# Attention scores in 32-row tiles without the q/k re-layout, hand-ordered attention engines, and a software-pipelined expert loop

## The chip, the cores and the metric

The kernel runs on one core of a Trainium2 chip. The core has TensorE (PE, with its weight loads PEld), VectorE (DVE), ScalarE (ACT), GpSimd (POOL) and SyncE (SP, which here only issues DMAs); 16 DMA engines serve all queues. Each engine works through its own instructions in order and waits on semaphores for the others. The metric is the device time of one execution in microseconds (us), lower is better.

## The reference

An attention layer with a sliding window feeds a mixture-of-experts layer.

- Attention: q, k, v are 8 x 8 x 576 x 64 (batch, head, position, depth), fp32. For each batch and head, `scores = q k^T / 8 - slope_h * |i - j|`, kept only where `0 <= i - j < 128`; softmax over j; times v. The result is laid out as 4608 tokens x 512.
- Experts: `y_dense = relu(x w1_dense) w2_dense` for every token; each token also goes to the one expert (of 8) with the largest gate logit, `y_moe = p_gate * (relu(x w1[e]) w2[e])`. The output is the sum, 4608 x 512 fp32.

## The kernel before

**Attention stage.** The work is cut into 16 units: a unit is one batch and four of its eight heads. Within a unit there are five key tiles of 128 positions. For key tile kj, `scores(u, kj)` puts the mask and bias into PSUM with a matmul against the identity (L266), adds q times k for the four heads (L275), and ACT takes the exponential into `p32` (L283). Scores are needed only for two query tiles, so a step is 4 heads x 256 queries = 1024 columns (768 and 256 for the last two key tiles). The values v and p are each split into a high and a low bf16 part: the high part of p is the upper half of its fp32 word, the low part `plo` is a DVE subtraction (L291). `attend(u, qi)` multiplies p by v in three products per head and key tile (L322) and DVE normalizes by the row sum, which comes from a column of ones in v (L330, L332). POOL casts the result to bf16 rows `xrow` (L342), PE transposes it (L350) and ACT copies it out (L357, L364).

Before its scores a unit needs q and k with depth on the partitions. POOL's queue loads q and k raw (L130), DVE transposes 32 x 32 blocks into `qs`, `ks` (L146), and SP's queue moves those in 16 DMAs per unit to `qT`, `kT` (L157), so that each head has its 64 depths on 64 neighbouring partitions. v comes over SP's queue (L138), ACT casts its high part (L167), POOL subtracts for the low part `vl` (L168).

After both units of a batch, `gate(b)` computes the expert choice of 576 tokens: PE products L378, L388, L419, L427 with some dozen DVE instructions of 40 columns between them (L396 to L447), and POOL scatters the rows by expert into DRAM (`xs_dram`, L456).

**Expert stage.** 43 blocks (NB) of 128 rows, each of one expert. Block j is fetched by POOL (L602), PE transposes it (L621), DVE copies (L625), PE makes the dense and the expert's first layer `hd` and `hm` (L630, L638; 8 matmuls of 512 columns), ACT applies relu (L646, L647), PE transposes the result (L651), DVE copies (L655, L656), PE makes the second layer `y` (L659, L667; 8 more), ACT copies it out (L675), and POOL scatters it to the output rows (L676). `tok_i` (L611), the output row numbers, needs the fetched block.

**What sets the order.** The program is written as a loop over steps with `LAG = 2` between `scores` and `attend`, but the order of each engine's instructions is chosen by a scheduler at compile time from the dependencies, within the buffer counts of the pools: two score buffers (`psum_sq`), two output buffers (`psum_ax`), four of `p32`. The two stages follow each other; the expert weights are loaded and cast by 18 DMAs of POOL's queue (L76) during attention.

The function, with the numbers that the profile uses:

Of the kernel before, what the change touches and what calls it, by code (L numbers as in the profile page):

```python
# [22 lines left out]
def kernel(  # L23
# [12 lines left out]
    nc = tc.nc  # L36
# [45 lines left out]
    kTs, vfs, vhs, lts = [], [], [], []  # L82
    for i in range(2):
        kT = persist.tile([P, 2, SP_], F32R, name=f"kT{i}")
        nc.gpsimd.memset(kT.bitcast(F32)[:, :, S:SP_], 0.0)
        kTs.append(kT)
        vf = persist.tile([P, NT, 4, D], F32, name=f"vf{i}")
        nc.gpsimd.memset(vf[TAIL:P, NT - 1, :, :], 0.0)
        vfs.append(vf)
        vh = persist.tile([P, NT, 4, D + 1], BF16, name=f"vh{i}")  # L90
        nc.gpsimd.memset(vh[:, :, :, D : D + 1], 1.0)
        vhs.append(vh)
# [6 lines left out]
    for i in range(1):  # L99
# [8 lines left out]
    ppool = ph1.enter_context(tc.tile_pool(name="ppool", bufs=4))  # L108
    xpool = ph1.enter_context(tc.tile_pool(name="xpool", bufs=2))
    gs = ph1.enter_context(tc.tile_pool(name="gs", bufs=3))  # L110
    psum_sq = ph1.enter_context(
        tc.tile_pool(name="psum_sq", bufs=2, space=bass.MemoryType.PSUM)
    )
    psum_ax = ph1.enter_context(
        tc.tile_pool(name="psum_ax", bufs=2, space=bass.MemoryType.PSUM)
# [9 lines left out]
    def load_unit(u):  # L125
        b, hq = divmod(u, HQ)
        hs = slice(4 * hq, 4 * hq + 4)
        for nm, src in (("q", q), ("k", k)):
            t = ld.tile([P, R, 2, 32], F32R, name=f"{nm}raw", tag=f"{nm}raw")
            nc.gpsimd.dma_start(  # L130
                out=t.rearrange("p r c d -> p (r c d)"),
                in_=src[b, hs].rearrange("h (p r) d -> (h p) (r d)", r=R),
            )
            raw[(nm, u)] = t
        vf = vfs[u % 2]
        for t in range(NT):
            rows = min(P, S - t * P)
            nc.sync.dma_start(  # L138
                out=vf[:rows, t, :, :],
                in_=v[b, hs, t * P : t * P + rows, :].rearrange("h p d -> p h d"),  # L140
            )

    def prep_qk(u, nm):
        t = raw.pop((nm, u))
        s = stg.tile([P, 2, S], F32, name=f"{nm}s", tag=f"{nm}s")
        nc.vector.transpose(  # L146
            out=s.rearrange("p c (x r) -> p r c x", r=R),
            in_=t.bitcast(F32),
        )
        if nm == "q":  # L150
            d = qtp.tile([P, 2, S], F32R, name="qT", tag="qT")
        else:
            d = kTs[u % 2]
        for g in range(4):
            pl, hh = divmod(g, 2)
            for c in range(2):
                nc.sync.dma_start(  # L157
                    out=d.bitcast(F32)[hh * D + 32 * c : hh * D + 32 * c + 32, pl, 0:S],
                    in_=s[32 * g : 32 * g + 32, c, :],
                )  # L160
        qkT[(nm, u)] = d

    def prep_v(u):
        vf = vfs[u % 2]
        vh = vhs[u % 2]
# [5 lines left out]
    load_unit(0)  # L171

# [37 lines left out]
    tok_c = consts.tile([P, NT], I32, name="tok_c")  # L210
    nc.gpsimd.iota(tok_c, pattern=[[P, NT]], base=0, channel_multiplier=1)
# [16 lines left out]
    mask = consts.tile([P, HQ, 2, 2, PW], BF16, name="mask")  # L228
    with tc.tile_pool(name="mk", bufs=1) as mk:
        d_i = mk.tile([P, PW], I32, name="d_i")  # L230
        nc.gpsimd.iota(d_i, pattern=[[1, PW]], base=0, channel_multiplier=-1)
        d_f = mk.tile([P, PW], F32, name="d_f")
        nc.vector.tensor_copy(out=d_f, in_=d_i)
        inv = mk.tile([P, PW], F32, name="inv")
        big = mk.tile([P, PW], F32, name="big")
        nc.vector.tensor_single_scalar(out=inv, in_=d_f, scalar=0.0, op=ALU.is_lt)
        nc.vector.tensor_single_scalar(
            out=big, in_=d_f, scalar=float(WINDOW - 1), op=ALU.is_gt
        )
        nc.vector.tensor_tensor(out=big, in0=inv, in1=big, op=ALU.add)  # L240
        nc.vector.tensor_scalar_mul(out=big, in0=big, scalar1=NEG_BIG)
        for h in range(H):
            hq, g = divmod(h, 4)
            pl, r = divmod(g, 2)
            slope = 2.0 ** (-8.0 * (h + 1) / H)
            nc.vector.scalar_tensor_tensor(
                out=mask[:, hq, r, pl, :],
                in0=d_f,
                scalar=-slope / SCALE,
                in1=big,  # L250
                op0=ALU.mult,
                op1=ALU.add,
            )


    pbuf = {}

    def scores(u, kj):
        hq = u % HQ
        k0 = kj * P  # L260
        nq = min(PW, S - k0)
        qT = qkT[("q", u)]
        kT = qkT[("k", u)]
        sq = psum_sq.tile([P, 2, 512], F32, name="sq", tag="sq")
        for r in range(2):
            nc.tensor.matmul(  # L266
                out=sq[:, r, 0 : 2 * nq],
                lhsT=ident_b,
                rhs=mask[:, hq, r, :, 0:nq],
                start=True,  # L270
                stop=False,
            )
        for pl in range(2):
            for r in range(2):
                nc.tensor.matmul(  # L275
                    out=sq[:, r, pl * nq : (pl + 1) * nq],
                    lhsT=kT[r * D : (r + 1) * D, pl, k0 : k0 + P],
                    rhs=qT[r * D : (r + 1) * D, pl, k0 : k0 + nq],
                    start=False,
                    stop=(pl == 1),  # L280
                )
# [7 lines left out]
        phi = p32.bitcast(BF16).rearrange("p r l (c t) -> p r l c t", t=2)[:, :, :, :, 1]
        plo = ppool.tile([P, 2, 2, PW], BF16, name="plo", tag="plo")  # L290
        nc.vector.tensor_tensor(  # L291
            out=plo[:, :, :, 0:nq],
            in0=p32[:, :, :, 0:nq],
            in1=phi[:, :, :, 0:nq],
            op=ALU.subtract,
        )
        pbuf[(u, kj)] = (phi, plo)
# [3 lines left out]
    def attend(u, qi):  # L301
        b, hq = divmod(u, HQ)
        rows = min(P, S - qi * P)
        vh, vl = vparts[u]
        ax = psum_ax.tile([P, 512], F32, name="ax", tag="ax")
        ax_v = ax[:, 0 : 4 * (D + 1)].rearrange("p (h d) -> p h d", h=4)
        for g in range(4):
            pl, r = divmod(g, 2)
            kl = [kj for kj in (qi - 1, qi) if kj >= 0]
            n = 0  # L310
            for kj in kl:
                phi, plo = pbuf[(u, kj)]
                c0 = 0 if qi == kj else P
                hi = phi[:, r, pl, c0 : c0 + rows]
                lo = plo[:, r, pl, c0 : c0 + rows]
                for lhs, rhs, w in (
                    (hi, vh[:, kj, g, :], D + 1),
                    (hi, vl[:, kj, g, :], D),
                    (lo, vh[:, kj, g, :], D + 1),
                ):  # L320
                    n += 1
                    nc.tensor.matmul(  # L322
                        out=ax_v[:rows, g, 0:w],
                        lhsT=lhs,
                        rhs=rhs,
                        start=(n == 1),
                        stop=(n == 3 * len(kl)),
                    )
        recip = gs.tile([P, 4], F32, name="recip", tag="recip")
        nc.vector.reciprocal(out=recip[:rows], in_=ax_v[:rows, :, D])  # L330
        xf = xpool.tile([P, 4, D], F32, name="xf", tag="xf", bufs=4)
        nc.vector.tensor_tensor(  # L332
            out=xf[:rows],
            in0=ax_v[:rows, :, 0:D],
            in1=recip[:rows].unsqueeze(2).to_broadcast([rows, 4, D]),
            op=ALU.mult,
        )
        if hq == 0 and qi == 0:
            cur["xT"] = xpool.tile([P, 4, SP_], F32, name="xT", tag="xT", bufs=1)
            cur["xrow"] = xpool.tile([P, NT, RW], BF16, name="xrow", tag="xrow", bufs=2)  # L340
        xT, xrow = cur["xT"], cur["xrow"]
        nc.gpsimd.tensor_copy(  # L342
            out=xrow[:rows, qi, hq * 256 : hq * 256 + 256],
# [370 lines left out]
```

## Time and profile before

| | |
|---|---|
| median of 3 runs | 598.61 us (597.23 to 600.31) |
| profiled execution | 603.1 us, span 601.4 us |
| busy in the span: PE / DVE / ACT / POOL | 76% / 50% / 32% / 45% |
| mean granted TensorE clock | 0.807 of 2.4 GHz |
| DMA | 76.36 MB, 127 GB/s over the span |

The span is the time between the first and the last instruction; the execution's own time is 1.7 us more. The busy share is an average over two very different stages: attention (to about 362 us) and the experts (from about 380 us). The stages have to be read apart.

### The profile page before, as it was taken

What the parts mean: (1) busy time and instruction counts of PE and PEld (TensorE: products, weight loads), DVE (VectorE), ACT (ScalarE), POOL (GpSimd) and SP (SyncE); (2) the same over time, 40 slices, a digit from 0 to 9 for tenths busy, and PEclk for the clock granted to TensorE, in tenths of its full rate; (3) what the DMA queues carried; (4) which work ended last, traced back from release to release, by engine and by line L of the source; (5) the groups of instructions that cost most, each with busy time, mean ns of one, the idle gap of its engine ahead of it and who ended that gap; (6) DMA issues with size and microseconds to landing.
All of it is one profiled execution on the core that took longest, in us unless ns stands there. A gap on an engine that the chain in (4) does not pass through costs nothing. (4 is left out here: it accounts for less than half of the span.)

```text
span 601.4 us, 10655 instructions
## 1 busy us (share of the span) xinstructions
PE 456.5 (76%) x3828; PEld 272.7 (45%) x3828; DVE 303.2 (50%) x554; ACT 193.0 (32%) x298; POOL 271.2 (45%) x366
## 2 busy tenths in 40 slices
PE   0476566977776776777778782699999999999992
PEld 0254343654544554545555461344444444444440
DVE  3746456687588668766786755122222222222220
ACT  1222223343134233432441431233333333333331
POOL 6362565474274264454552623544434444444432
PEclk9995666756776776676677696699999999999997
DMA  7899999785576557657556401121121211222110
GB/s 186 212 235 221 249 249 239 189 213 117 137 204 137 147 150 165 163 119 188 161 137 139 119 2 41 45 81 58 70 69 60 80 67 71 69 80 78 55 52 26
DMA packets 72418, 76.36 MB, mean 127 GB/s; under 512 B 46252, under 2 KB 55470, under 8 KB 72368
## 3 DMA queue, kind: packets, MB, share of 16 engines
q0 software_dynamic: 21408, 47.35, 30.6%
q1 hardware_dynamic: 50960, 28.35, 20.3%
q8 instruction: 31, 0.51, 0.4%
q14 instruction: 19, 0.16, 0.1%
HBM read 52.93 MB, written 16.06 MB: 115 GB/s over the span
## 5 line engine op out<-in xcount | busy, mean ns | idle before, releaser
L291 DVE TENSOR_TENSOR plo<-p 128x1024 bf16<-128x1024 f32 (+2 forms) x80 | 108.8, 1398 | 15.2 <-ACT p L283 15.2
L283 ACT ACTIVATE p<-sq 128x1024 f32<-128x1024 f32 (+2 forms) x80 | 66.3, 852 | 98.1 <-PE sq L275 87.4
L322 PE MATMUL ax<-vh,plo 128*128 128x65 bf16 (+1 forms) x576 | 89.0, 225 | 11.1 <-DVE plo L291 11.1
L625 DVE COPY xT<-xps 128x512 bf16<-128x512 bf16 x43 | 18.2, 423 | 156.2 <-PE xps L621 152.7
L322 PEld LDWEIGHTS <-p 128*128 128x128 bf16 (+1 forms) x1152 | 84.0, 122 | 23.6 <-issue 20.6
L266 PE MATMUL sq<-mask,ident_b 128*128 128x512 bf16 (+2 forms) x160 | 60.8, 478 | 42.0 <-ACT p L283 20.9
L322 PE MATMUL ax<-vh,p 128*128 128x65 bf16 (+1 forms) x576 | 90.4, 226 | 0.0
L322 PE MATMUL ax<-vl,p 128*128 128x64 bf16 (+1 forms) x576 | 89.9, 224 | 0.0
L342 POOL CAST xrow<-xf 128x256 bf16<-128x256 f32 (+1 forms) x80 | 44.4, 559 | 79.8 <-DVE xf L332 79.7
L322 PEld LDWEIGHTS <-plo 128*128 128x128 bf16 (+1 forms) x576 | 68.4, 122 | 22.6 <-DVE plo L291 17.8
L350 PE MATMUL tp<-ident_f,xf 128*128 128x128 f32 (+1 forms) x160 | 42.0, 354 | 43.1 <-DVE xf L332 42.4
L675 ACT COPY yo<-y 128x512 f32<-128x512 f32 x43 | 25.2, 585 | 131.0 <-PE y L667 124.9
L275 PE MATMUL sq<-qT,kT 64*128 64x256 f32 (+2 forms) x320 | 60.3, 405 | 6.1 <-DMA kT<-ks 4.4
L456 POOL DMA_INDIRECT xs_dram<-xrow,slot x40 | 46.5, 1164 | 33.2 <-DVE slot L441 14.1
L676 POOL DMA_INDIRECT out_dram<-yo,tok_i x43 | 43.6, 1014 | 36.9 <-issue 14.7
L275 PEld LDWEIGHTS sq<-qT,kT 64*128 64x128 f32 x320 | 42.2, 262 | 28.9 <-issue 20.5
L630 PE MATMUL hd<-w_all,xT 128*128 128x512 bf16 x172 | 52.3, 387 | 0.9 <-DVE xT L625 0.5
L168 POOL TENSOR_TENSOR vl<-vf,vh 128x1280 bf16<-128x1280 f32 x16 | 45.7, 2856 | 16.0 <-ACT vh L167 15.9
L602 POOL DMA_INDIRECT xr<-xs_dram,row_i x43 | 43.9, 1021 | 16.0 <-issue 14.7
L357 ACT COPY xT<-tp 128x512 f32<-128x512 f32 x32 | 18.7, 586 | 86.5 <-PE tp L350 86.5
L638 PE MATMUL hm<-w_all,xT 128*128 x172 | 45.0, 385 | 0.0
L659 PE MATMUL y<-w_all,hT 128*128 128x512 bf16 x172 | 44.1, 379 | 0.5 <-DVE hT L655 0.5
(109 smaller groups left out, 607.4 us busy)
## 6 DMA issues: line engine op xcount, KB each, us to landing
qraw<-in_q_dram POOLq DMA_DIRECT2D x16, 576.0 KB
kraw<-in_k_dram POOLq DMA_DIRECT2D x16, 576.0 KB
qT<-qs SPq DMA_DIRECT2D x128, 72.0 KB
kT<-ks SPq DMA_DIRECT2D x128, 72.0 KB
vf<-in_v_dram SPq DMA_DIRECT2D x64, 128.0 KB
w_all<-in_moe_w_dram POOLq DMA_DIRECT2D x16, 512.0 KB
vf<-in_v_dram SPq DMA_DIRECT2D x16, 64.0 KB
w_all<-in_moe_w_dense_dram POOLq DMA_DIRECT2D x2, 512.0 KB
```

What stands on the lines that cost most here:

```text
L168: nc.gpsimd.tensor_tensor(out=vl, in0=vf, in1=vh[:, :, :, 0:D], op=ALU.subtract)
L266: nc.tensor.matmul(out=sq[:, r, 0 : 2 * nq], lhsT=ident_b, rhs=mask[:, hq, r, :, 0:nq], start=True, stop=False,)
L275: nc.tensor.matmul(out=sq[:, r, pl * nq : (pl + 1) * nq], lhsT=kT[r * D : (r + 1) * D, pl, k0 : k0 + P], rhs=qT[r * D : (r + 1) * D, pl, k ...
L283: nc.scalar.activation(out=p32[:, :, :, 0:nq], in_=sq[:, :, 0 : 2 * nq].rearrange("p r (l c) -> p r l c", l=2), func=ACT.Exp, scale=SCALE,)
L291: nc.vector.tensor_tensor(out=plo[:, :, :, 0:nq], in0=p32[:, :, :, 0:nq], in1=phi[:, :, :, 0:nq], op=ALU.subtract,)
L322: nc.tensor.matmul(out=ax_v[:rows, g, 0:w], lhsT=lhs, rhs=rhs, start=(n == 1), stop=(n == 3 * len(kl)),)
L342: nc.gpsimd.tensor_copy(out=xrow[:rows, qi, hq * 256 : hq * 256 + 256], in_=xf[:rows].rearrange("p h d -> p (h d)"),)
L456: ins = nc.gpsimd.indirect_dma_start(out=xs_dram[:, :], out_offset=bass.IndirectOffsetOnAxis(ap=slot[:rows, t : t + 1], axis=0), in_=xrow_ ...
L602: nc.gpsimd.indirect_dma_start(out=xm_i[:, :], out_offset=None, in_=xs_dram[:, :], in_offset=bass.IndirectOffsetOnAxis(ap=row_i[:, j : j + ...
L630: nc.tensor.matmul(out=hd, lhsT=xT[:, kc, :], rhs=w_all[:, E, 0, kc, :], start=(kc == 0), stop=(kc == 3),)
L638: nc.tensor.matmul(out=hm, lhsT=xT[:, kc, :], rhs=w_all[:, bass.DynSlice(er, 1), 0, kc, :], start=(kc == 0), stop=(kc == 3),)
L659: nc.tensor.matmul(out=y, lhsT=hT[:, c, :], rhs=w_all[:, E, 1, c, :], start=(c == 0), stop=False,)
```

## The change

**Layout of q and k.** The 16 re-layout DMAs per unit go. A head's 64 depths are now summed in two passes over 32 partitions (c = 0, 1), with head g on partitions 32g to 32g+31, which is where the DVE transposes leave them; ACT copies `ks` to `kT` and `qs` to `qT` (L159, L167 of the new file). So that the tokens of one q tile fall into place, q is loaded in five DMAs, and q, k and v all come over SP's queue. The queries of a tile stand in another order, so the mask and the token numbers `tok_c` are built for that order.

**Two key tiles per step.** A unit has three steps, key tiles (0,1), (2,3) and (4). A step's scores go to two PSUM tiles `sq0`, `sq1` of two heads each, without a second buffer; the exponential and `plo` are done per pair of heads over 1024 columns. The normalization handles two query tiles at once (`ax`, one buffer). v's high part is read in place as the upper half of its fp32 word, and DVE makes `vl` (L174).

**Order by hand.** PE, ACT and DVE follow the order of the code in the attention stage. A step n is: scores of n, exponentials, `plo` of the first head pair, products and normalization of step n-1, `plo` of the second pair, then the transposes of the next unit's k (first step), q (second step) or v's low part (third step). `gate` is cut in three and spread over three steps.

**Expert loop.** PE, ACT, DVE and POOL follow the code. PE takes `turn_h(j)`, `layer1(j+1)`, `turn_x(j+2)`, `layer2(j)`; blocks are fetched four ahead; DVE instead of ACT copies `y` out.

On ACT, in one unit of attention, the scheduler's order before (five exponentials of a unit, the cast of v and a copy):

```order
L283 ACTIVATE p_2829<-sq 128x1024
L283 ACTIVATE p_2883<-sq 128x1024
L283 ACTIVATE p_2985<-sq 128x1024
L167 CAST vh_75<-vf_73 128x20x64
L283 ACTIVATE p_3033<-sq 128x4x192
L283 ACTIVATE p_3086<-sq 128x4x64
L357 COPY xT<-tp 128x2x2x128 x2
```

and the written order now, the three steps of a unit:

```order
L346 ACTIVATE p_1254<-sq_1232 128x1024
L346 ACTIVATE p_1257<-sq_1233 128x1024
L448 COPY xT<-tp 128x2x2x128
L159 CAST kT_70<-ks 128x2x576
L346 ACTIVATE p_1328<-sq_1306 128x1024
L346 ACTIVATE p_1331<-sq_1307 128x1024
L448 COPY xT<-tp 128x2x64
L167 CAST qT<-qs 128x1152
L346 ACTIVATE p_1403<-sq_1389 128x2x64
```

The casts of the next unit's k and q now stand between the exponentials of one step and those of the next.

On DVE, in a unit of attention, before (both transposes, then `plo` of three key tiles):

```order
L146 STREAM_TRANSPOSE ks<-kraw 128x18x64
L146 STREAM_TRANSPOSE qs<-qraw 128x18x64
L291 TENSOR_TENSOR plo<-p_2587 128x1024
L291 TENSOR_TENSOR plo<-p_2641 128x1024
L291 TENSOR_TENSOR plo<-p_2686 128x1024
L330 RECIPROCAL recip<-ax 128x4
L332 TENSOR_TENSOR xf<-ax,recip 128x256
```

and now (the first step and the second; the names p_1254 to p_1331 are those of the exponentials shown above):

```order
L365 TENSOR_TENSOR plo<-p_1254 128x1024
L410 RECIPROCAL recip<-ax 64x4
L412 TENSOR_TENSOR xf<-ax,recip 64x256
L365 TENSOR_TENSOR plo<-p_1257 128x1024
L157 STREAM_TRANSPOSE ks<-kraw 128x18x64
L365 TENSOR_TENSOR plo<-p_1328 128x1024
L410 RECIPROCAL recip<-ax 128x8
L412 TENSOR_TENSOR xf<-ax,recip 128x512
L365 TENSOR_TENSOR plo<-p_1331 128x1024
L165 STREAM_TRANSPOSE qs<-qraw 128x18x2x32
L365 TENSOR_TENSOR plo<-p_1403 128x2x64
```

The transpose of k has moved between the last `plo` of one step and the first of the next, that of q one step later.

On POOL, in the expert loop, before (`xr` with a number is one of five buffers of fetched blocks):

```order
L602 DMA xr_85<-xs_dram,row_i 128x260
L611 TENSOR_TENSOR tok_i<-xr_85,inval_i 128x1
L676 DMA out_dram<-yo,tok_i 4608x512
L602 DMA xr_77<-xs_dram,row_i 128x260
L611 TENSOR_TENSOR tok_i<-xr_77,inval_i 128x1
```

and now:

```order
L727 DMA xr_75<-xs_dram,row_i 128x260
L793 TENSOR_TENSOR tok_i<-xr_81,inval_i 128x1
L826 DMA out_dram<-yo,tok_i 4608x512
L727 DMA xr_77<-xs_dram,row_i 128x260
L793 TENSOR_TENSOR tok_i<-xr_83,inval_i 128x1
```

Before, `tok_i` reads the block whose fetch stands directly ahead of it; now one that was fetched three iterations earlier.

The diff, cut to its core:

```diff
 def load_unit(u):
...
+        t = ld.tile([P, R, 2, 32], F32, name="qraw", tag="qraw")
+        for i in range(NT):
+            n = 4 if i < NT - 1 else 2
+            nc.sync.dma_start(
+                out=t[:, 4 * i : 4 * i + n, :, :].rearrange("p r c d -> p (r c d)"),
+                in_=q[b, hs, i * P : i * P + 32 * n, :].rearrange(
+                    "h (p r) d -> h p (r d)", r=n),
+            )
...
-        for g in range(4):
-            pl, hh = divmod(g, 2)
-            for c in range(2):
-                nc.sync.dma_start(
-                    out=d.bitcast(F32)[hh * D + 32 * c : hh * D + 32 * c + 32, pl, 0:S],
-                    in_=s[32 * g : 32 * g + 32, c, :],
-                )
+    def transpose_k(u):
+        s = stg.tile([P, 2, S], F32, name="ks", tag="ks")
+        nc.vector.transpose(out=s.rearrange("p c (x r) -> p r c x", r=R), in_=t)
+        d = kTs[u % 2]
+        nc.scalar.copy(out=d[:, :, 0:S], in_=s)
...
-        nc.scalar.copy(out=vh[:, :, :, 0:D], in_=vf)
-        nc.gpsimd.tensor_tensor(out=vl, in0=vf, in1=vh[:, :, :, 0:D], op=ALU.subtract)
+        nc.vector.tensor_tensor(
+            out=vl, in0=vf[:, :, :, 0:D], in1=vh[:, :, :, 0:D], op=ALU.subtract)
...
+        for i, kj in enumerate(kjs):
+            nq = min(wid, S - kj * P)
+            for c in range(2):
+                for g in range(4):
+                    nc.tensor.matmul(
+                        out=sq[g // 2][:, g % 2, i * wid : i * wid + nq],
+                        lhsT=kT[32 * g : 32 * g + 32, c, kj * P : kj * P + P],
+                        rhs=qT[32 * g : 32 * g + 32, c, kj * P : kj * P + nq],
+                        start=False, stop=(c == 1 and i == len(kjs) - 1))
...
+    for n in range(NS + 6):
+        if n < NS:
+            lo = scores(u, pr)
+            lo(0)
+        if 1 <= n <= NS:
+            norms[n - 1] = attend(*steps[n - 1])
+            flips[n - 1] = norms.pop(n - 1)()
+        if lo is not None:
+            lo(1)
...
+            flip(*steps[n - 2], flips.pop(n - 2))
...
+            if pr == 0:
+                load_v(u + 1)
+                transpose_k(u + 1)
+            elif pr == 1:
+                transpose_q(u + 1)
+            else:
+                prep_v(u + 1)
+                if u + 2 < NU:
+                    load_unit(u + 2)
...
-            nc.scalar.copy(out=yo, in_=y)
+            nc.vector.tensor_copy(out=yo, in_=y)
...
+        AHEAD = 4
+        for j in range(AHEAD):
+            fetch(j)
+        turn_x(0)
+        layer1(0)
+        turn_x(1)
+        for j in range(NB):
+            turn_h(j)
+            if j + 1 < NB:
+                layer1(j + 1)
+            if j + 2 < NB:
+                turn_x(j + 2)
+            layer2(j)
+            if j + AHEAD < NB:
+                fetch(j + AHEAD)
```

## Rows read from the trace of the kernel before

**Rows 1.** Windows: stretch, length, busy of PE, PEld, DVE, ACT, POOL, clock, DMA, GB/s.
```profile
60.00:100.00 40.00, 25.29 (x236) 16.94 (x235) 21.05 (x39) 10.86 (x17) 22.91 (x28) 0.60 1.19 250
150.00:200.00 50.00, 37.45 (x404) 26.34 (x405) 35.75 (x58) 15.48 (x23) 21.12 (x28) 0.69 0.64 157
450.00:500.00 50.00, 48.36 (x290) 22.86 (x289) 11.78 (x30) 18.31 (x32) 21.77 (x30) 1.00 0.19 66
```

**Rows 2.** Timeline of DVE: k transposed, first and last of ten units.
```profile
140.77 2.34 DVE L146 STREAM_TRANSPOSE ks<-kraw 128x1152 f32<-128x1152 f32 x1
...
327.17 2.33 DVE L146 STREAM_TRANSPOSE ks<-kraw 128x1152 f32<-128x1152 f32 x1
```

**Rows 3.** Timeline of DVE: start and end of attention.
```profile
17.14 2.77 DVE L246 SCALAR_TENSOR_TENSOR mask<-d_f,big 128x256 bf16<-128x256 f32 x8
...
28.36 2.33 DVE L291 TENSOR_TENSOR plo<-p 128x1024 bf16<-128x1024 f32 x2
...
361.45 0.17 DVE L330 RECIPROCAL recip<-ax 64x4 f32<-64x4 f32 x1 [0.71 <-PE ax L322]
361.73 0.42 DVE L332 TENSOR_TENSOR xf<-ax,recip 64x256 f32<-64x256 f32 x1
```

**Rows 4.** Line L291: durations in ns, min/median/max over all its forms.
```profile
L291 DVE TENSOR_TENSOR plo<-p x80: 414/1208/4489, 28.4 to 358.0; 128x1024 bf16<-128x1024 f32 x48, 128x768 bf16<-128x768 f32 x16, 128x256 bf16<-128x256 f32 x16
```

**Rows 5.** Lines by form: busy us, mean ns of one, idle before.
```profile
L283 ACT ACTIVATE p<-sq 128x1024 f32<-128x1024 f32 x48 | 47.4, 1022 | 47.4 <-PE sq L275 43.5 <-ACT p L283 2.0 <-issue 2.0
...
L146 DVE STREAM_TRANSPOSE ks<-kraw 128x1152 f32<-128x1152 f32 x16 | 37.4, 2339 | 6.0 <-DMA kraw<-in_k_dram 5.7
...
L167 ACT CAST vh<-vf 128x1280 bf16<-128x1280 f32 x16 | 20.1, 1255 | 14.0 <-DMA kT<-ks 14.0
...
L283 ACT ACTIVATE p<-sq 128x256 f32<-128x256 f32 x16 | 6.1, 383 | 36.3 <-PE sq L275 32.1 <-DVE xf L332 2.4 <-DVE plo L291 1.9
...
L396 DVE TENSOR_REDUCE mx<-lg 128x5 f32<-128x40 f32 x8 | 1.6, 200 | 11.4 <-PE lg L388 11.4
```

**Rows 6.** Timeline of PE: four 64-row score matmuls; sixteen 32-column gate matmuls.
```profile
353.01 0.50 PE L275 MATMUL sq<-qT,kT 64*128 64x256 f32 x4
...
160.24 1.18 PE L378 MATMUL lp<-xT,wg_pad 128*32 128x288 f32 x16
```

**Rows 7.** Timeline, DVE and POOL: a plo beside POOL's vl.
```profile
147.37 3.55 DVE L291 TENSOR_TENSOR plo<-p 128x1024 bf16<-128x1024 f32 x1
...
146.53 3.32 POOL L168 TENSOR_TENSOR vl<-vf,vh 128x1280 bf16<-128x1280 f32 x1 [0.40 <-ACT vh L167]
```

**Rows 8.** Timeline of PE in the expert loop, one block and the next.
```profile
481.27 0.40 PE L651 MATMUL hps<-ident_b,hr 128*128 128x128 bf16 x4
...
483.01 1.03 PE L659 MATMUL y<-w_all,hT 128*128 128x512 bf16 x4
483.87 1.03 PE L667 MATMUL y<-w_all,hT 128*128 x4
...
487.82 1.03 PE L659 MATMUL y<-w_all,hT 128*128 128x512 bf16 x4
```

**Rows 9.** Timeline of POOL in the expert loop, from one output scatter to the next.
```profile
482.19 1.01 POOL L676 DMA_INDIRECT out_dram<-yo,tok_i  x1 [0.58 <-ACT hr L647]
...
486.36 0.18 POOL L611 TENSOR_TENSOR tok_i<-xr,inval_i 128x1 int32<-128x1 int32 x1 [1.83 <-DMA xr<-xs_dram,row_i]
487.12 1.02 POOL L676 DMA_INDIRECT out_dram<-yo,tok_i  x1 [0.58 <-ACT hr L647]
```

**Rows 10.** Timeline, PE and POOL: first and last work of the expert loop.
```profile
379.98 0.61 PE L621 MATMUL xps<-ident_b,xr 128*128 128x128 bf16 x4 [13.09 <-DMA xr<-xs_dram,row_i]
...
589.52 1.03 PE L667 MATMUL y<-w_all,hT 128*128 x4
...
588.98 0.98 POOL L676 DMA_INDIRECT out_dram<-yo,tok_i  x1 [2.51 <-DMA out_dram<-yo,tok_i]
...
597.87 0.98 POOL L676 DMA_INDIRECT out_dram<-yo,tok_i  x1 [4.52 <-issue]
```

More of the change, by code (lines that the diff above doesn't have):

```diff
@@ L289, in scores @@
[L289 to L297, printed above, removed]
-    cur = {}
[L301 to L343, printed above, removed]
-            in_=xf[:rows].rearrange("p h d -> p (h d)"),
-        )
-        if qi % 2 == 0:
-            cur["tp"] = psum_m.tile([P, 2, 2, P], F32, name="tp", tag="misc")
-        tp = cur["tp"]
-        for c in range(2):
-            nc.tensor.transpose(
-                out=tp[:, qi % 2, c, 0:rows],
-                in_=xf[:rows, 2 * c : 2 * c + 2, :],
-                identity=ident_f[:rows, :rows],
-            )
-        if qi % 2 == 1:
-            q0 = (qi - 1) * P
-            nc.scalar.copy(
-                out=xT[:, 2 * hq : 2 * hq + 2, q0 : q0 + PW].rearrange(
-                    "p c (t x) -> p t c x", t=2
-                ),
-                in_=tp,
-            )
-        elif qi == NT - 1:
-            nc.scalar.copy(
-                out=xT[:, 2 * hq : 2 * hq + 2, qi * P : qi * P + rows],
-                in_=tp[:, 0, :, 0:rows],
-            )
@@ new lines, in scores @@
+        ps = []
+        for i in range(2):
+            p32 = ppool.tile([P, 2, 2 * PW], F32, name="p32", tag="p32")
+            nc.scalar.activation(
+                out=p32[:, :, 0:tot],
+                in_=sq[i][:, :, 0:tot],
+                func=ACT.Exp,
+                scale=SCALE,
+            )
+            phi = p32.bitcast(BF16).rearrange("p g (c t) -> p g c t", t=2)[:, :, :, 1]
+            plo = ppool.tile([P, 2, 2 * PW], BF16, name="plo", tag="plo")
+            ps.append((p32, phi, plo))
@@ new lines, in flip @@
+    def flip(u, pr, xf):
+        b, hq = divmod(u, HQ)
+        qis = KP[pr]
+        rows = P if len(qis) == 2 else TAIL
+        nt = len(qis)
+        if hq == 0 and pr == 0:
+            cur[("xT", b)] = xpool.tile([P, 4, SP_], F32, name="xT", tag="xT", bufs=1)
+        xT = cur[("xT", b)]
+        tp = psum_m.tile([P, 2, 2, P], F32, name="tp", tag="misc")
+        for i in range(nt):
+            for c in range(2):
+                nc.tensor.transpose(
+                    out=tp[:, i, c, 0:rows],
+                    in_=xf[:rows, i, 2 * c : 2 * c + 2, :],
+                    identity=ident_f[:rows, :rows],
+                )
+        q0 = qis[0] * P
+        nc.scalar.copy(
+            out=xT[:, 2 * hq : 2 * hq + 2, q0 : q0 + nt * rows].rearrange(
+                "p c (t x) -> p t c x", t=nt
+            ),
+            in_=tp[:, 0:nt, :, 0:rows],
+        )
@@ L467, in gate @@
             tc.add_to_no_dep_group(scat_group, ins.ins)
-    steps = [(u, kj) for u in range(NU) for kj in range(NT)]
-    prep_qk(0, "q")
-    prep_qk(0, "k")
+    sch = ph1.enter_context(
+        tc.manual_schedule(
+            engines={
+                mybir.EngineType.PE,
+                mybir.EngineType.Activation,
+                mybir.EngineType.DVE,
+            }
+        )
+    )
+    steps = [(u, pr) for u in range(NU) for pr in range(3)]
+    transpose_k(0)
+    transpose_q(0)
@@ L472 @@
     prep_v(0)
     load_unit(1)
[L474 to L495 removed]
+    norms, flips, later = {}, {}, {}
```

426 lines of the change are left out of this document (281 added, 145 removed).

## The prediction, made before the changed kernel ran

> **What bounds the kernel now.** I read the windows first, because the span falls into two stages that no mean describes. In the expert loop PE works 48.4 of 50 us at a granted clock of 1.00; in attention 37.5 of 50 us at 0.69, with DVE at 35.8 and no engine full [rows 1]. Only the lower and the upper level (1.2 and 2.4 GHz) are granted there, in turn.
>
> Then the timeline. In the expert loop the y matmuls of one block start 4.81 us after those of the block before [rows 8]. The whole loop runs from 379.98 to 590.55 us, 210.6 us [rows 10]: 43 blocks x 4.81 = 206.8, and 3.8 to fill it. POOL is as slow as PE there: from one output scatter to the next are 4.93 us, because `tok_i` waits for the block whose fetch was issued just ahead of it [rows 9], and at the end POOL is behind, with its last scatter at 597.87 us, 7.3 us after PE's last matmul [rows 10].
>
> In attention the transposes of k mark the units: nine units in 186.4 us, 20.7 us each [rows 2]. The first `plo` begins at 28.36 us and the last normalization ends at 362.15 [rows 3].
>
> The profiled execution took 603.1 us (span 601.4), the median of the runs shown is 598.6, 4.5 less. I make the sum on the profiled execution and take the difference over to the runs.
>
> **The expert loop, the surest part.** Its matmuls are the same before and after: 16 of 512 columns per block and 12 transposes. Four y matmuls take 0.86 us from start to start (483.01 to 483.87), so one takes 0.216; four transposes take 0.40 us, of which the last one alone shows 0.22, so one takes 0.06 [rows 8]. 16 x 0.216 + 12 x 0.06 = 4.18 us of PE in a block of 4.81: 0.63 us are waits for relu and for copies. In the new order every such wait has other work in front of it: relu of block j+1 has `turn_x` and `layer2(j)` (0.24 + 1.73 us) against the two relus that follow the last matmul of the layer by less than 1 us; the DVE copy of `turn_h(j)` has `layer1(j+1)` (1.73 us). On DVE a block's copies are about 0.8 + 0.4 + 0.7 us, on ACT only the two relus are left. On POOL the `tok_i` wait goes; what is late next there is the chain of output scatters, each of which waits for the landing of the one before: 2.51 + 0.98 = 3.49 us where they follow one another closely [rows 10], less than 4.2. I take 4.2 us per block and 4.5 to fill (one stage more): 43 x 4.2 + 4.5 = 185.1, a gain of **25.5 us**. Bounds: 0 if something else keeps 4.8 us; 27 if no wait is left.
>
> The tail: now 10.8 us pass between PE's last matmul and the end of the span (590.55 to 601.4), since POOL is behind. If it isn't behind, there remain a copy (0.7), a scatter and what follows a last scatter now (597.87 to 601.4, 3.5 us): about 5, or up to 9 if the 4.52 us of "issue" before the last scatter [rows 10] come again. I take 6, a gain of **5 us**.
>
> **Attention, where the gain is doubtful.** What goes: 16 re-layout DMAs per unit and POOL's `vl`. With `vl` goes a wait: a `plo` beside it took 3.55 us [rows 7] against a median of 1.21 [rows 4]. What comes: two ACT casts of 1152 columns per unit, `vl` on DVE, and a fixed order. The fixed order makes a chain that can be followed: DVE transposes k, then ACT casts it, and only behind this cast stands the next step's first exponential, for which DVE's next `plo` waits. I add one unit up along DVE, with handovers of 0.06 us:
>
> - First step: `plo` 1.21; normalization 0.70 (reciprocal start to the end of xf, 361.45 to 362.15 [rows 3]); `plo` 1.21; transpose of k 2.34 [rows 5]: 5.5. Then DVE waits for the cast, 1.15 (estimate from 1.255 for 1280 columns), and the exponential, 1.02 [rows 5], with handovers 2.3.
> - Second step: `plo` 1.21; normalization of 512 columns instead of 256, about 1.0; `plo` 1.21; transpose of q 2.34: 5.8. Wait for the cast and a small exponential (0.28, estimate from 0.383 for 256 columns): 1.5.
> - Third step: two small `plo` 0.3 each, normalization 1.0, `vl` 1.5 (estimate from 1.21 for 1024 columns): 3.1. Meanwhile PE makes the next scores, which had to wait until ACT had emptied `sq0` and `sq1`, as these have no second buffer: four mask matmuls (0.9 at the upper clock, twice that at the lower), four rounds of scores (1.0 to 2.0) and the exponential 1.02: 2.9 to 4.8. DVE waits up to 1.7; I take 0.8.
> - The gate: 13 DVE instructions of about 0.2 us [rows 5] per two units and some waits: 1.5 per unit. POOL's cast beside `vl`: 0.2.
>
> The sum is 20.7 us, and about 20.5 if back-to-back `plo` overlap a little: what the unit takes now. The removed DMAs and the smaller number of instructions are paid back by 3.8 us of new waiting behind the casts. Bounds of one unit: 18 (no wait after the third step, faster casts) and 22.5.
>
> What hides the other edits: q's five loads and v's five are 0.6 us each to issue on SP, which loses 16 issues per unit. PE's fp32 transposes and products are the same in number; they stand in the shadow of DVE's transposes. v's high part is now read with a stride of two bf16: if that slowed the products, some 2 us per unit of PE, this would be hidden there too, except in the third step.
>
> Total: the first exponential had to wait for q and k through SP's DMAs; now the masks are last (8 of 512 columns instead of 256: 5 us instead of 2.77 [rows 3]), so the first `plo` comes at about 24 us instead of 28.4 (between 21 and 29). Units 0 and 1 have no gate before them: 2 x 19; units 2 to 14: 13 x 20.5 = 266.5; the last has nothing to prepare: 10.7. Sum 315, so the end is at 339. While the expert weights stream in, DMA is full (share 1.19, [rows 1]); all 18 are now issued from the start, beside the loads that the transposes need. I add 6 us: 345 instead of 362.15, a gain of **17 us** (bounds: 40, and a loss of 20).
>
> Gate, routing and first fetch, 17.8 us between 362.15 and 379.98, stay.
>
> **Sum.** 25.5 + 5 + 17 = 47.5: 603.1 becomes 555.6, and the runs 598.6 become **551**.
>
> **A rule weighed.** The four tiles must work at the same time. The trace has two tiles of 64 rows: four matmuls of 256 columns in 0.50 us, while one alone shows 0.4; and sixteen gate matmuls that use 32 columns of the array each in 1.18 us [rows 6], four at a time. So I count a round of four like a round of two, 0.25 us. The Trainium skill (TensorE: Matmul & The Clock Gate, "Measured speedup vs the span model") gives 3.07 times, not 4, for four row tiles. By that a round would take 0.33 us; only the four rounds after the third step are exposed, 0.3 us per unit and 5 us in all: 556. No run here shows it yet.
>
> **The rivals.**
>
> *Faster attention (14%).* ACT's and DVE's pieces are shorter than my estimates and PE is granted the upper clock, so that the third step's wait vanishes: 18.4 us per unit, 15 x 2.1 = 31 us more: 520. For it: DVE and ACT together are far from full [rows 1]. Against: the order is a chain, not a load.
>
> *Loads late (16%).* While weights stream, q and v of the next unit are late; DVE stands in the transpose with everything behind it. Five units at 5 us more: 576. For it: the DMA share of 1.19 and PE at only 25 of 40 us in that stretch [rows 1]. Against: k, q and v no longer share POOL's queue with the weights, and no re-layout competes.
>
> *The expert loop stays (8%).* The change doesn't do what it says: the scatter chain or the register loads for the expert number keep 4.8 us per block: 25.5 and the tail come back, 582. Against: 3.49 us per scatter.
>
> *Slower: the tiles take turns (7%).* If the four row tiles run one after another, a round of 0.25 us becomes 1.0 and the 10 rounds of a unit cost 7.5 us more of PE at the upper clock, 15 at the lower. PE has about 5 of 20.7 us free now (37.5 of 50 busy, [rows 1]). So a unit gets 2.5 to 10 us longer; with 6, 15 x 6 = 90 us: 641. It decides from 3.2 us per unit on, where the 47.5 are used up. Against: rows 6.
>
> **How the numbers follow.** The forecast has 55%, with a range of its own of 537 to 567 (a unit of 19.7 to 21.5). With most of the cases at 520, 576 and 582 the range of 8 in 10 is 521 to 582. The measurement can tell about 0.5% (3 us) from no change. Faster: 55 + 14 + 16 + 8 less the ends of the wide cases, 91%; same 2%; slower 7%.
>
> **What would show it.** In the new profile: y matmuls of successive blocks 4.2 us apart; PE's last matmul within 6 us of the end; ks transposes 20.5 us apart; between a transpose of k and the next `plo` about 2.3 us in which ACT does a cast and an exponential; four score matmuls of 256 columns in 0.25 to 0.35 us at the upper clock. I am wrong if DVE waits for DMA in steady units, if PE's rounds take turns, or if the unit is under 19 us.

## The result, and the profile after

The changed kernel takes 563.07 us (median of 4 runs, 560.39 to 563.8), the kernel before 598.5: a ratio of 0.940 (95% interval 0.936 to 0.944). The forecast was 551 us, with a range of 521 to 582. The time lies in the range, 12 us above the point. One run of an experiment below (the new loop under the old attention, 579.0 us) fell in a slower state of the chip and is left out of its time.

The profiled execution took 560.4 us (span 558.7). Cut at the same places as the forecast:

| stretch | forecast, us | measured, us |
|---|---|---|
| start to the first `plo` | 24 | 28.0 |
| units 0 and 1 | 38 + 6 for loads | 63.8 |
| units 2 to 13, each | 20.5 | 18.7 |
| unit 14 and the last | 31.2 | 29.6 |
| end of attention at | 345 | 345.65 |
| gate, routing, first fetch | 17.8 | 18.35 |
| expert loop | 185.1 | 184.6 |
| PE's last matmul to the end | 6 | 10.05 |

The end of attention was met to 0.65 us, and not because its terms were right: the first units are 20 us too long, the steady ones 22 us too short.

The windows of the changed kernel (columns as in [rows 1]), a stretch with weights, a steady one, and the expert loop:

```profile
15.00:60.00 45.00, 20.32 (x208) 13.12 (x207) 19.51 (x26) 9.42 (x12) 13.81 (x21) 0.90 1.21 218
150.00:200.00 50.00, 31.74 (x465) 24.50 (x462) 36.12 (x60) 21.27 (x34) 16.58 (x18) 0.76 0.37 107
450.00:500.00 50.00, 50.00 (x340) 27.06 (x339) 20.55 (x36) 15.41 (x24) 27.14 (x37) 1.00 0.27 91
```

In the first row DMA is full (1.21) and DVE works 19.5 of 45 us. In the second the DMA share has fallen to 0.37 from the 0.64 of [rows 1], DVE has about the same work in 50 us, and no engine is full. In the third PE has no gap left.

The transposes of k mark the units, as in [rows 2]. Timeline of DVE:

```profile
30.26 2.33 DVE L157 STREAM_TRANSPOSE ks<-kraw 128x1152 f32<-128x1152 f32 x1
63.34 2.32 DVE L157 STREAM_TRANSPOSE ks<-kraw 128x1152 f32<-128x1152 f32 x1
94.04 2.32 DVE L157 STREAM_TRANSPOSE ks<-kraw 128x1152 f32<-128x1152 f32 x1
113.23 2.34 DVE L157 STREAM_TRANSPOSE ks<-kraw 128x1152 f32<-128x1152 f32 x1
131.15 2.33 DVE L157 STREAM_TRANSPOSE ks<-kraw 128x1152 f32<-128x1152 f32 x1
```

Unit 0 takes 33.1 us, unit 1 30.7, and from unit 2 on they take 17.9 and 19.6 in turn (the gate's work falls into every second). What DVE waits for in units 0 and 1 stands in brackets in its timeline, with SP's queue below (start, duration of the issue; five loads of v or q each). For the first of the three waits the profile names no releaser ("issue"); the transpose behind it needs q's five loads, which SP had issued only by 28.2 us:

```profile
43.72 1.38 DVE L165 STREAM_TRANSPOSE qs<-qraw 128x1152 f32<-128x1152 f32 x1 [5.79 <-issue]
...
59.12 1.49 DVE L174 TENSOR_TENSOR vl<-vf 128x1280 bf16<-128x1280 f32 x1 [11.30 <-DMA vf<-in_v_dram]
...
84.19 1.38 DVE L165 STREAM_TRANSPOSE qs<-qraw 128x1152 f32<-128x1152 f32 x1 [13.11 <-DMA qraw<-in_q_dram]
```

```profile
28.26 18.23 SPq L149 DMA_DIRECT2D vf<-in_v_dram  x5
...
58.10 17.81 SPq L135 DMA_DIRECT2D qraw<-in_q_dram  x5
...
104.04 2.88 SPq L135 DMA_DIRECT2D qraw<-in_q_dram  x5
```

Five issues that take SP 2.88 us in a steady unit take 18 while the weights stream, those of q (packets of 1024 bytes) as long as those of v (256 bytes). DMA by queue, 45 to 50 us (packets, MB, share of 16 engines), when v's loads meet the weights:

```profile
q0 software_dynamic: 787, 0.78, 91.4%
q1 hardware_dynamic: 793, 0.20, 30.0%
```

The weights' queue and SP's moved nearly the same number of packets in these 5 us, and SP's are a quarter as large. It is not so throughout: at 25 to 30 us, with q's loads on SP's queue, it is 934 packets to 155. And the engines are not full throughout: at 70 to 80 us, while DVE waits for q, the DMA share is 0.34.

A steady unit, DVE and then ACT:

```profile
225.41 2.34 DVE L157 STREAM_TRANSPOSE ks<-kraw 128x1152 f32<-128x1152 f32 x1
229.89 1.23 DVE L365 TENSOR_TENSOR plo<-p 128x1024 bf16<-128x1024 f32 x1 [2.14 <-ACT p L346]
...
234.57 1.38 DVE L165 STREAM_TRANSPOSE qs<-qraw 128x1152 f32<-128x1152 f32 x1
237.34 0.29 DVE L365 TENSOR_TENSOR plo<-p 128x128 bf16<-128x128 f32 x1 [1.39 <-ACT p L346]
```

```profile
227.78 1.15 ACT L159 CAST kT<-ks 128x1152 fp32r<-128x1152 f32 x1 [2.48 <-DVE ks L157]
228.84 1.93 ACT L346 ACTIVATE p<-sq 128x1024 f32<-128x1024 f32 x2
...
235.98 1.15 ACT L167 CAST qT<-qs 128x1152 fp32r<-128x1152 f32 x1 [5.06 <-DVE qs L165]
237.04 0.44 ACT L346 ACTIVATE p<-sq 128x128 f32<-128x128 f32 x2
```

This is the chain that was forecast: transpose, cast, exponential, `plo`, with waits of 2.14 and 1.39 us (forecast 2.3 and 1.5). ACT had been idle for 2.48 and 5.06 us ahead of the casts, though PE had finished the scores at 224.2 and 231.7 us. The transpose of q takes 1.38 us, not the 2.34 of k.

The expert loop, PE and POOL, against [rows 8, 9]:

```profile
482.70 1.03 PE L817 MATMUL y<-w_all,hT 128*128 x4
...
486.83 1.03 PE L817 MATMUL y<-w_all,hT 128*128 x4
```

```profile
481.14 1.01 POOL L826 DMA_INDIRECT out_dram<-yo,tok_i  x1 [1.56 <-DVE hT L757]
482.46 1.03 POOL L727 DMA_INDIRECT xr<-xs_dram,row_i  x1 [0.30 <-ACT hr L791]
483.51 0.20 POOL L793 TENSOR_TENSOR tok_i<-xr,inval_i 128x1 int32<-128x1 int32 x1
485.27 1.01 POOL L826 DMA_INDIRECT out_dram<-yo,tok_i  x1 [1.56 <-DVE hT L757]
```

4.13 us per block instead of 4.81, and `tok_i` waits for nothing. The end of the kernel (PE's last matmul, POOL's last scatter, then the group of POOL's drains, DRAIN instructions that stand at its end; min/median/max in ns):

```profile
547.61 1.03 PE L817 MATMUL y<-w_all,hT 128*128 x4
```

```profile
550.13 0.97 POOL L826 DMA_INDIRECT out_dram<-yo,tok_i  x1 [2.27 <-DVE yo L825]
```

```profile
L875 POOLq DRAIN  x3: 51/103/7968, 549.9 to 558.4; - x3
```

The last scatter is now early, but POOL's last drain takes 7.97 us; before, the same drain took 2.69 and the last scatter came late by 4.52 us of "issue" [rows 10].

### The profile page after: what moved, and what is told of

The parts are those of the page before. It is cut to its first block, busy times and chain, and to the rows that moved or that the text cites. A ratio compares the mean times of both kernels' runs of the same rounds, so it can differ in the third digit from the quotient of the medians.

```text
span 558.7 us, 10709 instructions
## 1 busy us (share of the span) xinstructions
PE 393.9 (70%) x4180; PEld 254.5 (46%) x4180; DVE 308.8 (55%) x536; ACT 186.4 (33%) x287; POOL 216.6 (39%) x288
## 4 chain that ended last, share of the span: by engine, by line
PE 37%; DVE 26%; DMA 12%; SPq 9%; issue 8%; ACT 6%; POOL 1%; DVEq 0%; POOLq 0%; ACTq 0%
DVE plo L365 11%; ACT p L346 6%; PE y L809 5%; PE y L817 5%; DVE ks L157 5%; PE hm L774 5%; SPq L135 5%; PE hd L782 5%; SPq L149 4%; DMA vf<-in_v_dram 4%; PE ax L399 3%; DMA out_dram<-yo,tok_i 3%; DVE xf L412 3%; PE sq L325 3%; DMA xr<-xs_dram,row_i 2%
## 5 line engine op out<-in xcount | busy, mean ns | idle before, releaser
L325 PE MATMUL sq<-mask,ident_b 128*128 128x512 bf16 (+1 forms) x192 | 46.3, 347 | 113.6 <-ACT p L346 90.3
L423 POOL CAST xrow<-xf 128x512 bf16<-128x512 f32 (+1 forms) x48 | 54.8, 1143 | 183.7 <-DVE xf L412 183.7
L365 DVE TENSOR_TENSOR plo<-p 128x1024 bf16<-128x1024 f32 (+1 forms) x96 | 88.0, 917 | 65.4 <-ACT p L346 65.0
L399 PE MATMUL ax<-vf,p 128*128 128x65 bf16 (+1 forms) x576 | 81.8, 222 | 16.4 <-DVE xf L412 16.4
L399 PE MATMUL ax<-vf,plo 128*128 128x65 bf16 (+1 forms) x576 | 81.3, 219 | 5.2 <-DVE plo L365 4.9
L346 ACT ACTIVATE p<-sq 128x1024 f32<-128x1024 f32 (+1 forms) x96 | 68.9, 769 | 33.0 <-PE sq L336 33.0
L325 PEld LDWEIGHTS <-ident_b 128*128 128x128 bf16 x192 | 19.1, 105 | 128.8 <-issue 109.5
L790 ACT ACTIVATE hr<-hm,xr 128x512 bf16<-128x512 f32 x43 | 29.5, 687 | 133.7 <-PE hm L774 131.1
L825 DVE COPY yo<-y 128x512 f32<-128x512 f32 x43 | 29.7, 691 | 58.0 <-PE y L817 58.0
L744 DVE COPY xT<-xps 128x512 bf16<-128x512 bf16 x43 | 18.2, 424 | 58.3 <-PE xps L740 58.3
L167 ACT CAST qT<-qs 128x1152 fp32r<-128x1152 f32 x16 | 18.4, 1152 | 85.8 <-DVE qs L165 85.8
L817 PE MATMUL y<-w_all,hT 128*128 x172 | 44.1, 379 | 0.0
L159 ACT CAST kT<-ks 128x1152 fp32r<-128x1152 f32 x16 | 18.4, 1152 | 64.2 <-DVE ks L157 64.2
```

The lines of the kernel that those rows point to most:

```text
L325: nc.tensor.matmul(out=sq[g // 2][:, g % 2, 0:tot], lhsT=ident_b, rhs=rhs, start=True, stop=False,)
L346: nc.scalar.activation(out=p32[:, :, 0:tot], in_=sq[i][:, :, 0:tot], func=ACT.Exp, scale=SCALE,)
L365: nc.vector.tensor_tensor(out=plo[:, :, 0:tot], in0=p32[:, :, 0:tot], in1=phi[:, :, 0:tot], op=ALU.subtract,)
L399: nc.tensor.matmul(out=ax[:rows, i, o0 : o0 + w], lhsT=lhs, rhs=rhs, start=(n == 1), stop=(n == 3 * len(kl)),)
L423: nc.gpsimd.tensor_copy(out=xrow[:rows, qis[0] : qis[0] + nt, hq * 256 : hq * 256 + 256], in_=xf[:rows, 0:nt].rearrange("p t h d -> p t (h ...
L817: nc.tensor.matmul(out=y, lhsT=hT[:, 4 + c, :], rhs=w_all[:, bass.DynSlice(er, 1), 1, c, :], start=False, stop=(c == 3),)
```

## The experiments

Each kernel is compared with runs of the kernel before on the same chip, so ratios are what compares; the changed kernel's is 0.940. Distances between transposes of k, from the traces (the first holds the start, the next two are units 0 and 1):

| kernel | start | unit 0 | unit 1 | mean of units 2 to 13 |
|---|---|---|---|---|
| before | 14.1 | 19.2 | 27.0 | 21.2 |
| changed | 26.0 | 33.1 | 30.7 | 18.7 |
| weights paced | 21.2 | 17.1 | 17.2 | 18.7 |
| casts late | 26.5 | 32.0 | 30.5 | 15.4 |
| both | 21.6 | 13.7 | 13.8 | 16.2 |
| both, and two more | 20.8 | 14.7 | 14.3 | 15.7 |
| half packets | 26.6 | 20.4 | 31.9 | 19.2 |

**Weights paced.** The program asks for the weights in units 2 to 12, but POOL is not in the hand-ordered set, and the scheduler issues them from 5.9 to 50.3 us (in the kernel before, from 15.2 to 94.8). The memset makes each load wait for its unit.

```diff
     def load_weights(e):
+        nc.vector.memset(w_all[:, e, :, 0, 0:2], 0.0)
         for wi in range(2):
```

Expected: 

> The changed kernel, but each expert's weight loads are tied to a two-element memset that DVE does at the place where the program asks for the load (units 2 to 12), so that the 18 loads no longer start at 6 to 50 us. Theory A, the weights crowd q's and v's loads out of the DMA engines in the first units: the distances between the first transposes of k fall from 26, 33 and 31 us to 18 to 20, the DMA share from 1.2 to under 0.8, and the time from 563 to about 533 us (530 to 537). Rival B, the loads of the first units are late because q's five and v's five issues stand in one queue of SP: the distances stay at 26 to 33 us, and the time within 5 us of 563. Rival C, the crowding only moves to later units: the first three get short, units 2 to 12 get 2 to 3 us longer each, and the time is 553 to 563.

Measured: 527.49 us, ratio 0.877 (0.871 to 0.882). The window of 15 to 60 us:

```profile
15.00:60.00 45.00, 31.45 (x388) 21.06 (x388) 35.55 (x46) 17.07 (x23) 7.07 (x8) 0.85 0.37 102
```

DMA share 0.37 for 1.21, DVE 35.6 us for 19.5. Units 0 and 1 get 16.0 and 13.5 us shorter, the start 4.8; the later units, which now run beside the weights, keep their 18.7 us on average (DMA share 0.72 at 150 to 200 us). Theory A holds in its cause, and B and C fall; its size was too small, since the time lies 2.5 us below its range of 530 to 537 and units 0 and 1 below 18 us. What the same pacing would bring to the kernel before, whose unit 1 takes 27.0 us, was not run.

**Casts late.**

```diff
-        nc.scalar.copy(out=d[:, :, 0:S], in_=s)      # likewise for q
+        casts.append((d[:, :, 0:S], s))
 ...
             lo = scores(u, pr)
+            cast_pending()
             lo(0)
```

Expected: 

> The changed kernel, but ACT's casts of k and of q stand behind the exponentials of the next step instead of ahead of them. Theory A, the chain of the prediction (transpose, cast, exponential, plo): the 2.14 us that DVE waits after k's transpose and the 1.40 us after q's lose the cast's 1.15 each, a steady unit goes from 18.75 to 16.4 to 17 us, and the time from 563 to 536 to 543. Rival B, DVE's wait moves to the third step, since the next unit's scores now wait for q's cast: the unit stays within 0.5 us of 18.75 and the time at 555 to 565. Rival C, half of each: the unit at 17.5 to 18, the time at 547 to 553.

Measured: 519.26 us, ratio 0.863 (0.857 to 0.868), below the lowest range given (536 to 543). In the unit that starts at 216.7 us, ACT:

```profile
216.07 1.94 ACT L353 ACTIVATE p<-sq 128x1024 f32<-128x1024 f32 x2 [0.90 <-PE sq L343]
219.06 1.15 ACT L159 CAST kT<-ks 128x1152 fp32r<-128x1152 f32 x1 [1.05 <-DVE ks L164]
```

and DVE:

```profile
216.70 2.32 DVE L164 STREAM_TRANSPOSE ks<-kraw 128x1152 f32<-128x1152 f32 x1
218.88 1.20 DVE L372 TENSOR_TENSOR plo<-p 128x1024 bf16<-128x1024 f32 x1
```

The `plo` follows the transpose with no wait. Theory A counted the cast alone (1.15 us per wait) as given back; the exponential behind it also goes, since ACT does it while DVE transposes. Both waits vanish whole, 3.5 us, and the unit falls by 3.3. What is left is mainly the wait in the third step (0.5 to 0.7 us, 1.9 in units with a gate).

**The old loop under the new attention, and the new loop under the old.** In the first the section behind the routing is that of before, in the second that of after.

Expected: 

> The changed kernel's attention with the expert loop of before (order left to the scheduler, copy of yo on ACT, tok_i behind the fetch). Theory, the loop's share of the gain is its own: the loop takes 4.8 us per block again instead of 4.15, 25 to 27 us more, 588 to 591 us. Rival, part of the loop's gain comes from somewhere else (the weights being in place sooner, another first fetch): 563 to 583.

Expected: 

> The kernel before with only the changed expert loop. Theory, the two parts of the change add up: the loop at 4.15 us per block, 598.5 less 26 gives 571 to 574, and attention's own share of the change is the other 9 to 11 us. Rival, the old attention hands over later or leaves POOL behind, so the loop gains less: 580 to 590.

Measured: 591.37 us, ratio 0.984 (0.978 to 0.990), 0.4 us above the theory's range, and 571.01 us, ratio 0.949 (0.941 to 0.956), in its range. The y matmuls, first and last start of 172, in the old and in the new loop:

```profile
L788 PE MATMUL y<-w_all,hT x172: 379/379/379, 372.8 to 575.3; 128*128 x172
```

```profile
L696 PE MATMUL y<-w_all,hT x172: 379/379/380, 388.0 to 562.5; 128*128 x172
```

A block's fourth y matmul of these starts 0.65 us after its first; less that, 42 distances give 4.81 and 4.14 us. The loop's gain is its own, and the parts multiply within the noise: 0.984 x 0.949 = 0.934 against 0.940. Of the change's 6%, the loop brings some 5 and attention 1.6. Which edit within the loop or within attention brings how much was not run apart.

**Both edits.**

Expected: 

> Both edits of the first two experiments: weight loads tied to the unit that asks for them, and ACT's casts behind the next step's exponentials. Theory, loads that are late (units 0 to 2) and the cast chain (every unit) are separate causes and add: 563 less 35.6 less 43.8 gives 484 us (478 to 490), a steady unit of 15.4 us. Rival, the faster units now meet the weight loads, which are spread over units 2 to 12: these units stay at 17 to 18 us and the time at 500 to 515.

Measured: 487.56 us, ratio 0.815 (0.811 to 0.818): as the theory says, 4 us above its point. The causes are separate. Three units of the twelve take 17.8 to 18.3 us, and in these the rival is right: DVE waits for q's load, 3.30, 2.66 and 2.80 us, each time after POOL issued two pairs of weight loads some 6 us apart (84.5 and 90.7, 149.5 and 155.7, 214.2 and 220.3 us). The first of these waits, on DVE:

```profile
110.11 1.38 DVE L173 STREAM_TRANSPOSE qs<-qraw 128x1152 f32<-128x1152 f32 x1 [3.30 <-DMA qraw<-in_q_dram]
```

**Both, and two more.** At the start, k's transpose comes ahead of the constants, the masks of four heads ahead of q's transpose, and unit 0's `vl` and the other four masks behind the first two `plo`. The gate's matmuls come a step earlier (the cut shows this one):

```diff
-                later.setdefault(n + 1, []).append(lambda b=b: gate_a(b))
+                gate_a(b)
```

Expected: 

> The kernel with both edits and two more: DVE's first steps in the order transpose of k, constants, four of the eight masks, transpose of q, so that DVE no longer idles for q's load before it makes the masks (first plo at 18 to 20 us instead of 23.3); and the gate's matmuls directly behind the last flip of a batch instead of ahead of the next scores (the wait of 1.85 us in units behind a gate falls to the 0.6 of the others, seven times). Theory: 484 less 4 less 9 gives 471 us (465 to 478). Rival, neither lies on the path, since DVE makes the other masks later and the gate's copies only move on ACT: 480 to 488.

Measured: 482.21 us, ratio 0.805 (0.801 to 0.809), the fastest kernel of the study, but 5 us gained for 13 expected: the time lies in the rival's range, not the theory's. The first `plo` begins at 19.15 us instead of 23.56, as expected, but DVE makes the other masks right behind it, and the next transpose of k comes only 0.6 us earlier (25.24 for 25.84). The rest, 4.8 us, comes between there and the last unit's transpose. There units 2 to 13 get 6.4 us shorter, since in units with a gate the wait in the third step is 0.7 us or less and no longer 1.2 to 1.7; units 0 and 1 get 1.6 us longer, with a longer wait at the same place (1.6 and 1.2 us for 0.6 and 0.5). The two edits weren't run apart.

**One tile twice in a row.**

```diff
-            for c in range(2):
-                for g in range(4):
+            for g in range(4):
+                for c in range(2):
```

Expected: 

> The changed kernel, with the two depth passes of one head next to each other, so that two successive score matmuls use the same 32-row tile. Theory, tiles overlap only with a neighbour in another tile: the 16 score matmuls of a step, whose first and last start 0.45 us apart at the upper clock (four rounds of 0.11), then need ten slots of 0.11, 1.0 to 1.2 us (twice that at the lower clock); this shows in the third step alone, 0.6 to 1.2 us per unit, and the time goes from 563 to 573 to 580 us. Rival A, the tiles overlap in any order: 0.45 us and no change. Rival B, the tiles take turns in either order: 0.45 us would then already be the price of 16 matmuls one after another, and nothing changes either.

Measured: 562.98 us, ratio 0.941 (0.937 to 0.945): no change. Sixteen score matmuls of the changed kernel, and of this one, at the upper clock:

```profile
275.83 0.75 PE L336 MATMUL sq<-qT,kT 32*128 32x256 f32 x16
```

```profile
295.41 0.75 PE L336 MATMUL sq<-qT,kT 32*128 32x256 f32 x16
```

The first and last of the sixteen start 0.47 us apart in the changed kernel and 0.48 in this one (the 0.45 of the expectation was read too low). Rival A holds. B does not: at 512 columns in 0.216 us (the rate of the y matmuls, [rows 8]), sixteen matmuls of 256 columns one after another would take 1.7 us.

**Half packets.**

```diff
-                out=w_all[:, e, wi, :, :],
+                out=w_all[:, e, wi, :, fs],   # two loads, fs = columns 0:256 and 256:512
```

Expected: 

> The changed kernel, with each weight load split into two loads of half the columns, so that its packets are 512 bytes instead of 1024 and POOL issues 162 DMAs instead of 144. Theory A, DMA engines serve the weights' queue and SP's queue packet by packet in turn (45 to 50 us: 787 packets of the one and 793 of the other): a short packet of v then waits for half as long, v's load of a unit takes some 12 us instead of 18, the first three units take 18 to 24 us instead of 26 to 33, later ones more, and the time is 545 to 556. Rival B, the engines share by bytes or the sum of work counts: the first three units stay at 26 to 33 us and the time at 560 to 575. On the tail: if POOL's last drain (7.97 us, 2.7 in the kernel before) depends on the number of DMAs that POOL has issued, it changes; if on something else, it stays 7.97.

Measured: 554.88 us, ratio 0.929 (0.924 to 0.933). Five loads of v on SP's queue, as in the row at 28.26 us of the changed kernel:

```profile
25.20 12.39 SPq L151 DMA_DIRECT2D vf<-in_v_dram  x5
```

12.39 us for 18.23: shorter packets of the weights let SP's loads through sooner, in the proportion that theory A gave (12 for 18), q's too (12.38 for 17.81), and the time is in its range, with 1.8 us of the gain due to the last drain. But units 0 to 2 take 20.4, 31.9 and 26.1 us and not 18 to 24: the weights now stream until about 105 us instead of 80, so the crowding is milder and lasts longer. Nor do the queues always take turns one to one: 1347 packets of the weights to 733 of SP at 45 to 50 us here. The rule by which they share stays open. The last drain takes 6.17 us, so it does change.

**Thirty small DMAs,** four bytes each, added to the kernel of 482.21 us and issued by POOL in the first 30 us.

Expected: 

> The fastest kernel so far (482 us, weights paced, casts behind, new start and gate place) with 30 more DMAs of four bytes that POOL issues in the first 30 us and nobody reads, 174 instead of 144 POOL DMAs. Theory, POOL's last drain (7.97 us with 144 DMAs, 6.17 with 162) depends on how many DMAs POOL has issued: 18 more took 1.8 us, so 30 more take about 3 us, a drain of 4.9 to 5 us, and the time is 479 us. Rival, it depends on the packets or descriptors (162 DMAs had twice as many packets for the weights): the drain stays at 7.97 us and the time at 482.

Measured: 484.22 us, ratio 0.810 (0.805 to 0.815), which its interval does not tell from 0.805. The drain takes 8.54 us, neither 4.9 nor 7.97. So the number of POOL's DMAs alone doesn't set it (174 here, and 2.69 us with the 176 of the kernel before), nor does the number of packets (twice as many for the weights came with a shorter drain, 30 more with a longer one); its cause stays open.

## Why the prediction came out as it did

**The loop** (25.5 us): right in mechanism and size; 184.6 us for 185.1, and the loop alone shows 4.14 us per block under the old attention too.

**The tail** (5 us): the step that failed. The term that was mis-sized is "what follows a last scatter", taken as the 3.5 us of [rows 10]: it is 8.6 us (550.13 to 558.7), and 10.05 from PE's last matmul, above the bound "up to 9" too. The difference comes with the drain, 7.97 us for 2.69. The new loop under the old attention shows the other form (POOL):

```profile
567.03 0.98 POOL L705 DMA_INDIRECT out_dram<-yo,tok_i  x1 [4.90 <-issue]
```

```profile
L754 POOLq DRAIN  x3: 51/103/2683, 566.8 to 570.3; - x3
```

With the old attention the last scatter comes late by 4.5 to 4.9 us of "issue" and the drain takes 2.7 us, under either loop; with the new attention there is no such wait and the drain takes 7.97, under either. So it goes with attention's part of the change. That the wait before the scatter turned into the drain fits this, but isn't shown. From PE's last matmul to the end, the new loop has 7.6 us under the old attention and 10.05 under the new.

**Attention** (17 us; 16.5 between the two profiled runs): the right sum of two wrong terms. The medians give attention less, some 9.5 us (the ratio of 0.984): the profiled run before was 4.5 us above its median, and the end of the kernel got longer with the new attention.
- *Loads late*, a rival at 16%, is what happened, and harder than priced: not five units at 5 us but two units at 14 to 16 us beyond the paced kernel's, and 4.8 us at the start. The step that failed is "I add 6 us". What the forecast set against this rival, that k, q and v no longer share POOL's queue with the weights, didn't protect them: a queue of their own still shares the DMA engines. The profile had the full engines in view [rows 1]. The pacing experiment shows that the early weight loads are the cause, and that with the half packets that the size of their packets matters; how the engines divide their time between the two queues isn't shown.
- *Faster attention*, a rival at 14%, is true of the steady units: 18.7 us for its 18.4, and by the forecast's own sign ("the unit is under 19 us") its term of 20.5 is wrong. Of the rival's reasons one holds, pieces of DVE that are shorter than estimated; the other, a wait in the third step that vanishes, doesn't, since that wait is 0.06 and 1.86 us in turn in the later units. The transpose of q was priced by the row of k, 2.34 us, and takes 1.38. Both read and write the same 1152 elements; only the order in which the output is written differs, and before, with k's order, q took 2.34 too. That is 1 us of the 1.8; most of the rest is overlap: an instruction of DVE starts some 0.08 us before the one ahead of it ends (a `plo` of 1.23 us at 229.89, the next instruction at 231.03), some ten times per unit, 0.7 to 0.8 us, which the sum took at 0.2 us in all.
- The cast chain was right: two waits of 2.14 and 1.39 us. What I did not see is that its price could be had back whole by an order in which the exponential comes first.

**Four tiles at a time** was right, and better than taken: the second round starts 0.22 us after the first and each later one some 0.117 after the one before, where the sum took 0.25 for each. The rows it used [rows 6] show two rounds and so only the first, longer distance. The Trainium skill (TensorE: Matmul & The Clock Gate, "Measured speedup vs the span model") gives 3.07 times for four row tiles; here four matmuls of 256 columns take 0.117 us from one later round to the next, and one, by the rate of 512 in 0.216, 0.108: some 3.7 times, as an estimate. The slower rival, tiles that take turns, falls with it.

**From the profiled run to the median** I took 4.5 us off, since before lay so. After, the median lies 2.7 us above the profiled run. Of the 12 us between forecast and time, 4.8 are the sum's (4 of them the tail) and 7.2 this step: a difference between one profiled run and a median did not carry over, and no run shows a cause for it.

## What to carry to other kernels

Where some engines are ordered by hand and others by a scheduler, look at what the scheduler does with the loads: here it issued by 50 us 18 loads that the program asks for in units 2 to 12, and a two-element memset on a hand-ordered engine was worth 36 us. In a hand-written order, put a step that others only need later (a cast for the next unit) behind the one that the busiest engine waits for now; this was worth 44 us. And compare a forecast with the result term by term: a sum that comes out right can hide two errors of 20 us.

## What the runs showed of the hardware

- Loads wait beside those of another queue, and less so when the packets of those are smaller: v's five loads took SP 18.2 us beside weights in packets of 1024 bytes, 12.4 beside packets of 512. q's, in packets of 1024 bytes themselves, took 17.8 and 12.4. The Trainium skill (DMA: Bandwidth & Descriptors, "Queues, rings and completion order") says that each DMA engine takes turns, packet by packet, between the queues that it has work for, and that such a packet is a group of some 9 to 17 descriptors; whether the profile counts the same packets isn't shown. 787 to 793 of them in 5 us would fit turns of one each, 934 to 155 in the same kernel and 1347 to 733 in another would not by themselves.
- DVE's transpose of 1152 elements per partition takes 2.33 us where its output is written with a stride and 1.38 where runs of 32 are written in order.
- The order in which tiles are addressed does not matter to four row tiles: sixteen matmuls start within 0.47 and 0.48 us.
- POOL's last drain takes from 2.68 to 8.54 us, and no run explains it.
